# Linear attention and two mixtures of experts in one kernel: reciprocals' copies on VectorE, short tiles behind the queries' turn, and the rounding of weights spread and moved at the end of the attention

## Chip, core and metric

The kernel runs on one core of a Trainium2 chip. Its engines are TensorE (PE, with its weight loads as PEld), VectorE (DVE), ScalarE (ACT) and GpSimd (POOL); SyncE (SP) issues transfers. Each engine works through its own instructions in order and waits by semaphores for the others. The metric is the device time of one execution in microseconds, the median of several runs; less is better.

## What is computed

Three stages follow each other: a linear attention over 4 batches, 8 heads, 576 positions and 64 dimensions; a dense layer whose hidden part is the largest of three products; and a layer of 8 experts, of which each token takes two.

```python
def phi(x):                                   # attention
    proj = np.einsum('bhsd,df->bhsf', x, w_phi)
    proj = proj - np.max(np.abs(proj), axis=-1, keepdims=True)
    return np.concatenate([np.exp(proj), np.exp(-proj)], axis=-1)
q_p, k_p = (phi(q), phi(k))
kv = np.einsum('bhsf,bhsd->bhfd', k_p, v)
num = np.einsum('bhsf,bhfd->bhsd', q_p, kv)
den = np.einsum('bhsf,bhf->bhs', q_p, np.sum(k_p, axis=2))[..., None] + 1e-06
x = num / den
...
h = np.maximum(np.maximum(x @ w1, x @ w2), x @ w3)
x = h @ w_out                                 # first layer, 512 -> 768 -> 512
...
out[mask] += top2_w[mask, k, None] * (np.maximum(x[mask] @ w1[e], 0.0) @ w2[e])
```

## The kernel before

The attention runs in 16 steps, one for two heads of one batch. A step `a` takes its keys and queries through these stations: `turn` transposes them on TensorE (L373), `raw_in` copies the result (ScalarE), `proj` multiplies by `w_phi` (L394), `peak` and `center` find and subtract the largest absolute value (VectorE, L404 and L419), `exp_k` makes the exponentials of the keys (ScalarE), `turn_q` transposes the queries' once more (L437) and `exp_q` makes theirs (L446). Then `kv_sum` (L465) adds up keys by values into one PSUM bank, `kv_out` copies it to SBUF (ScalarE, L470), `denom` (L498) and `numer` (L481) multiply it by the queries' exponentials, and `den_in`, `den_turn`, `den_inv`, `den_copy`, `den_back` and `divide` make and apply the reciprocals. The denominators come in 32 partitions for each half of the positions, and `den_copy` copies each group of reciprocals to the neighbouring group, which needs them too: four small instructions a step on ScalarE (L526).

Of each head's 576 positions 512 lie in main tiles. The other 64 of two batches share a short tile, marked "r", which is worked on in the even steps; its exponentials (L427) are used in the even step and the next.

Beside this, the weights of the first layer are rounded in 24 pieces of 128 x 512 that come from DRAM as 64-bit numbers. A piece `n` is loaded by `narrow_load` (L170, into one of two buffers that it shares with all later weights, `raw`), `narrow_mid` does two VectorE instructions (L179, L181) and one on ScalarE (`nr`, L184), `narrow_end` four on GpSimd (L192 to L195), and `narrow_out` writes it to DRAM again (L205) or, for the first block, splits it in place. `nm` has three buffers and `nr` two. `step_halves(a)` says which pieces a step takes: one each from step 1, two in steps 4, 6, ..., 14, and the rest behind the last step.

What stands where is given by hand: `at(t, f, ...)` records a call at a planned time (a step is 12.5 long), the calls are sorted by this number and made in that order, and on TensorE, VectorE, ScalarE and SP the instructions keep the order of the calls. The numbers are an order, not a wait. `period(base, a, b)` does this for the second half of step `b` and the first of `a`; the seam to the first layer is written out behind it, with `pe(duration, f, ...)` moving a clock along TensorE's work. At the seam the order is: the last two sums, `numer`, the block `first(0, 0, 0)` (12 matmuls), `denom`, `numer`, the next block, and so on; `larger` and `hidden` empty its PSUM banks (three). The weights of the next blocks are loaded by `w1_load` (L216) and split by `w1_split` into `wh` (ScalarE) and `wl` (VectorE, both in a helper, L121 and L122).

Of the kernel before, what the change touches and what calls it, by code (L numbers as in the profile page):

```python
# [12 lines left out]
I32 = mybir.dt.int32  # L13
U32 = mybir.dt.uint32
AF = mybir.ActivationFunctionType
ALU = mybir.AluOpType
# [3 lines left out]
P = 128  # L20
# [3 lines left out]
class Plan:  # L24
# [5 lines left out]
    def at(self, t, f, *x):  # L30
        self.ops.append((t, len(self.ops), f, x))
# [7 lines left out]
def tile_linear_attention__then__moe__then__noisy_top2_moe(  # L39
# [20 lines left out]
    nc = tc.nc  # L60
# [9 lines left out]
    JT = S // P  # L70
# [20 lines left out]
    at = plan.at  # L91
    st, pools = {}, {}
# [16 lines left out]
    def bank_k():  # L109
        return ps.tile([P, 512], F32, name="k", bufs=1)  # L110
# [60 lines left out]
        st["bits", n] = bits  # L171

    def narrow_mid(n):
        if ("bits", n) not in st:
            return
        bits = st["bits", n]
        low, high = bits[:, :, 0], bits[:, :, 1]
        m_ = pools["attn"].tile([P, 512], I32, name="nm", bufs=3)
        nc.vector.tensor_scalar(m_, high, 0x07ffffff, 3, op0=ALU.bitwise_and,  # L179
                                op1=ALU.logical_shift_left)  # L180
        nc.vector.scalar_tensor_tensor(m_, high, -0x40000000, m_, op0=ALU.bitwise_and,  # L181
                                       op1=ALU.bitwise_or)
        r_ = pools["attn"].tile([P, 512], I32, name="nr", bufs=2)
        nc.scalar.activation(r_, low.bitcast(U32), AF.Copy, scale=float(2.0 ** -29))  # L184
        st["nm", n] = r_, m_
# [170 lines left out]
    def heads(s):  # L356
        u, i = divmod(s, 2)
        bb, hp = divmod(u, HP)
        return u, i, bb, hp
# [93 lines left out]

    def kv_sum(s, h, part=None):
        u, i, bb, hp = heads(s)
        if h == 0 and part != 1:
            st["pkv"] = bank_k().rearrange("p (a f) -> p a f", a=4)

        order = [(sg, j) for sg in range(2) for j in range(JT)] + [(0, JT), (1, JT)]
        for sg, j in (order if part is None else order[JT:] if part else order[:JT]):  # L460
            if j < JT:
                kp, vv = kps[s][:, j % 2, 2 * h + j // 2, sg, :], tiles[s][2][:, j, h:h + 2, :]
            else:
                kp, vv = kps[u, "r"][:, h, sg, :], vls[i][:, hp, h:h + 2, :]
            nc.tensor.matmul(st["pkv"][:, 2 * h + sg, :], kp, vv.rearrange("p a d -> p (a d)"),  # L465
                             start=(j == 0 and sg == 0), stop=(j == JT and sg == 1))
# [21 lines left out]
    def quarter(h, n):  # L488
        g = 2 * h + n
        return slice(g * QD, (g + 1) * QD)  # L490
# [31 lines left out]
    def den_copy(s, n):  # L522

        rc = st["rc", s]
        for h in range(2):
            nc.scalar.activation(rc[quarter(h, 1 - n), n, :], rc[quarter(h, n), n, :], AF.Copy)  # L526

    def den_back(s, n):
        rb = ap.tile([P, NB, 32], F32, name="rb", bufs=2)
# [9 lines left out]
    NS = B * HP  # L539
    STEP = 12.5  # L540
# [35 lines left out]
    def step_halves(a):  # L576

        def count(a):
            return min(a, 1) + (a % 2 == 0 if a > 2 else 0)

        n = sum(count(i) for i in range(a))
        return range(n, n + count(a) if a < NS else len(halves))

    def period(base, a, b):

        def at(t, f, *x):
            plan.at(base + t, f, *x)

        if 0 < a < NS:
            at(0.0, fill, a)  # L590
            if a == 3:
                at(0.0, routing_loads)
            if a == 2:
                at(2.0, routing_consts)
            if a + 1 < NS:
                at(0.0, load_main, a + 1)
                at(0.0, load_vals, a + 1)
        if a < NS and a % 2 == 0:
            at(0.0, prepare, a)
        if 1 < a < NS:  # L600
            if a + 1 == 2 * HP:
                at(0.0, load_rest, 1)
            at(0.0, turn, a, "k")
            at(0.5, raw_in, a, "k")
            at(2.7, turn, a, "q")
            at(3.2, raw_in, a, "q")
            at(3.15, proj, a, "k")
            at(4.0, peak, a, "k", 0)
            at(4.7, center, a, "k", 0)
            at(5.4, peak, a, "k", 1)  # L610
            at(6.1, center, a, "k", 1)
            for g in range(2):
                for sg in range(2):
                    at(5.3 + 1.5 * g + 0.6 * sg, exp_k, a, "k", g, sg)
            at(7.25, proj, a, "q")
        if 0 < a < NS:
            at(8.1, peak, a, "q", 0)
            at(8.8, center, a, "q", 0)
            at(9.5, peak, a, "q", 1)
            at(10.2, center, a, "q", 1)  # L620
            at(9.95, turn_q, a, "q", 0)
            at(10.5, exp_q, a, "q", 0)
            at(11.05, turn_q, a, "q", 1)
            at(11.5, exp_q, a, "q", 1)
            if a % 2 == 0:
                at(2.8, turn, a, "r")
                at(3.4, raw_in, a, "r")
                at(11.4, proj, a, "r")
                for g in range(2):
                    at(11.5 + 0.01 * g, peak, a, "r", g)  # L630
                    at(11.52 + 0.01 * g, center, a, "r", g)
                at(STEP + 3.0, turn_q, a, "r", 0)
                at(STEP + 3.1, exp_q, a, "r", 0)
                at(12.39, exp_k, a, "r", 0, 0)
                at(12.39, exp_k, a, "r", 0, 1)
        if a < NS:
            for n in step_halves(a):
                at(1.8 if a > 1 else 11.0, narrow_mid, n)
                at(2.8 if a > 1 else 11.5, narrow_end, n)
                at(STEP + (1.6 if a > 1 else 9.0), narrow_out, n)  # L640
            for n in step_halves(a + 1):
                at(8.0, narrow_load, n)
            if a:
                at(10.5, kv_sum, a, 0, 0)
        if 0 < b:
            at(4.05, numer, b - 1, 1)
            at(6.9, divide, b - 1, 1)
            at(0.45, kv_sum, b, 0, 1)
            at(5.0, kv_sum, b, 1)
            if b + 1 == 2 * HP:  # L650
                at(7.3, load_rest_v, 1)
            at(7.3, kv_out, b)
        if 0 <= b:
            at(8.15, denom, b)
            at(9.1, numer, b, 0)
            at(9.15, den_in, b)
            at(10.9, den_turn, b)
            at(11.0, den_inv, b)
            for n in range(2):
                at(11.2 + 0.1 * n, den_copy, b, n)  # L660
                at(11.8 + 0.5 * n, den_back, b, n)
            at(11.9, divide, b, 0)

# [46 lines left out]
    for s in range(NS):  # L710
        period(s * STEP, s, s - 1)
    T = NS * STEP
# [470 lines left out]
    def pe(dur, f, *x):  # L1183
        at(clock[0], f, *x)
        clock[0] += dur

    def after(d, f, *x):
        at(clock[0] + d, f, *x)
# [8 lines left out]
    B0 = (NS - 1) * STEP  # L1197
    at(B0 + 10.6, open_m1)
    S_ = NS - 1
    pe(1.3, kv_sum, S_, 0, 1)  # L1200
    pe(0.96, numer, S_ - 1, 1)
    at(T + 0.3, split_x, 0, 0)
    after(0.5, divide, S_ - 1, 1)
# [8 lines left out]
    for n in range(2):  # L1212
        after(1.2 + 0.1 * n, den_copy, S_, n)
        after(1.8 + 0.5 * n, den_back, S_, n)
# [2 lines left out]
    first_pe(0, 0, 1)  # L1217
    pe(0.96, numer, S_, 1, bank_p)
    after(0.6, divide, S_, 1)
    for n in step_halves(NS):  # L1220
        at(T + 3.5, narrow_mid, n)
        at(T + 4.5, narrow_end, n)
        at(T + 11.0, narrow_out, n)
    END = clock[0] + 1.9
    at(END, open_rest)
    at(END + 1.6, routing_split)
    for i in range(2 * 4):
        g, j = 1 + i // 4, i % 4
# [230 lines left out]
```

## Time and profile before

| | |
|---|---|
| median of 3 runs | 1028.51 us (1027.62 to 1028.98) |
| the profiled execution, whole | 1027.36 us |
| its span, first to last instruction | 1025.8 us |
| TensorE busy | 999.5 us, 97% of the span |
| VectorE, ScalarE, GpSimd busy | 483.1, 380.8, 336.4 us |
| mean granted TensorE clock | 0.992 of full speed |

Times in the profile run from the first instruction. The attention's steps fill the time to about 217 us, one step takes 13 to 14 us. Busy time of matmuls includes the end of their pipeline, so neighbours overlap. A row of the timeline has the start, the busy time, the engine, the line, what is written and read, how many instructions of the kind follow each other, and in brackets the idle time before it with whom it waited for. A row of a stretch has its bounds and length, then busy us and number of instructions of PE, PEld, DVE, ACT and POOL, the granted clock, the share of the DMA engines and GB/s.

### The profile page before, as it was taken

How to read it: one execution, taken by the hardware profiler on the slowest of the kernel's cores; microseconds unless marked ns; L12 is line 12 of the kernel's file. 1: busy time of each engine (PE TensorE's matmuls, PEld its weight loads, DVE VectorE, ACT ScalarE, POOL GpSimd, SP SyncE). 2: the span in 40 equal slices, each digit the busy share in tenths (PEclk: the TensorE clock that was granted, in tenths of full speed). 3: DMA queues.
4: the chain of work that ended last, by engine and by line, in shares of the span. 5: the costliest groups of instructions: out<-in, count | busy, mean ns of one | idle time of the engine just before them, and what ended most of it. 6: DMA issues, size and time to landing. Idle time of an engine off the chain costs nothing. (4 is left out here: it accounts for less than half of the span.)

```text
span 1025.8 us, 16323 instructions
## 1 busy us (share of the span) xinstructions
PE 999.5 (97%) x6429; PEld 874.1 (85%) x6429; DVE 483.1 (47%) x962; ACT 380.8 (37%) x733; POOL 336.4 (33%) x385
## 2 busy tenths in 40 slices
PE   9999999969999999999999999999999999999995
PEld 7777777749999999999998789898898979898883
DVE  5777777755342423334255536444454434444220
ACT  6677666643231313122234424333231413233110
POOL 2677655551002020202032646142332415151301
PEclk9999999989999999999999999999999999999998
DMA  7546765425000000000225347354253535352200
GB/s 196 145 132 167 217 185 170 124 73 154 21 32 1 31 1 32 1 31 1 73 68 182 79 141 253 130 155 145 92 165 98 165 117 185 113 175 80 75 19 31
DMA packets 78592, 109.25 MB, mean 106 GB/s; under 512 B 33422, under 2 KB 47886, under 8 KB 78514
## 3 DMA queue, kind: packets, MB, share of 16 engines
q1 hardware_dynamic: 67586, 78.57, 25.7%
q0 software_dynamic: 10928, 29.62, 8.7%
q8 instruction: 51, 0.84, 0.4%
q14 instruction: 27, 0.22, 0.1%
HBM read 84.77 MB, written 23.98 MB: 106 GB/s over the span
## 5 line engine op out<-in xcount | busy, mean ns | idle before, releaser
L993 PE MATMUL s<-gx,wh 128*128 128x304 f32 (+1 forms) x960 | 209.2, 309 | 0.1
L993 PEld LDWEIGHTS s<-gx,wh 128*128 128x128 f32 x960 | 159.0, 188 | 3.7 <-DVE gx L122 0.6
L993 PE MATMUL s<-gx,wl 128*128 128x304 f32 (+1 forms) x480 | 148.2, 309 | 0.0
L745 PE MATMUL s<-xh,wh 128*128 128x384 f32 x432 | 147.5, 341 | 0.0
L745 PE MATMUL s<-xh,wl 128*128 128x384 f32 x432 | 145.4, 337 | 0.0
L745 PE MATMUL s<-xl,wh 128*128 128x384 f32 x432 | 145.2, 336 | 0.0
L1081 POOL DMA_INDIRECT out_dram<-o,emeta x40 | 43.2, 1079 | 245.4 <-DVE o L1079 235.2
L922 POOL DMA_INDIRECT meta<-mt,si x36 | 35.4, 984 | 258.9 <-DVE a L755 247.8
L755 DVE TENSOR_TENSOR a<-s,a 128x384 f32<-128x384 f32 x72 | 40.1, 557 | 151.6 <-PE s L745 145.1
L1003 ACT ACTIVATE hh<-s 128x304 fp32r<-128x304 f32 (+1 forms) x120 | 52.3, 435 | 155.5 <-PE s L993 139.8
L1004 DVE SCALAR_TENSOR_TENSOR hl<-s,hh 128x304 fp32r<-128x304 f32 (+1 forms) x120 | 58.3, 488 | 100.4 <-ACT hh L1003 83.6
L122 DVE TENSOR_TENSOR wl<-raw,wh 128x1024 fp32r<-128x1024 f32 x72 | 88.1, 1224 | 36.3 <-ACT wh L121 35.6
L121 ACT ACTIVATE wh<-raw 128x1024 fp32r<-128x1024 f32 x72 | 76.0, 1056 | 55.5 <-DMA raw<-in_moe_w_dram 20.4
L993 PEld LDWEIGHTS s<-gx,wl 128*128 128x128 f32 x480 | 90.6, 189 | 1.4
L1071 PE MATMUL p<-wh,hh 128*128 128x512 f32 (+1 forms) x216 | 87.0, 403 | 0.0
L1071 PE MATMUL p<-wl,hh 128*128 128x512 f32 (+1 forms) x216 | 85.0, 394 | 0.0
L1071 PE MATMUL p<-wh,hl 128*128 128x512 f32 (+1 forms) x216 | 84.9, 393 | 0.0
L745 PEld LDWEIGHTS s<-xh,wh 128*128 128x128 f32 x432 | 81.1, 188 | 2.9 <-issue 0.5
L745 PEld LDWEIGHTS s<-xl,wh 128*128 128x128 f32 x432 | 81.2, 188 | 1.5
L745 PEld LDWEIGHTS s<-xh,wl 128*128 128x128 f32 x432 | 81.1, 188 | 0.0
L465 PEld LDWEIGHTS k<-vt,kp 128*128 128x128 f32 x512 | 60.8, 192 | 6.9 <-issue 6.5
L465 PE MATMUL k<-vt,kp 128*128 128x128 f32 x512 | 66.4, 278 | 0.1
(221 smaller groups left out, 1740.9 us busy)
## 6 DMA issues: line engine op xcount, KB each, us to landing
raw<-in_moe_w_dram SPq DMA_DIRECT2D x64, 512.0 KB, 3.5
bits<-in_moe_w_dram SPq DMA_DIRECT2D x18, 512.0 KB, 4.2
out_dram<-zrow SPq DMA_DIRECT2D x9, 512.0 KB, 5.2
x2d<-x SPq DMA_DIRECT2D x18, 256.0 KB, 2.1
km<-in_k_dram SPq DMA_DIRECT2D x16, 256.0 KB, 5.1
qm<-in_q_dram SPq DMA_DIRECT2D x16, 256.0 KB, 5.1
vt<-in_v_dram SPq DMA_DIRECT2D x32, 128.0 KB, 4.8
narrow<-nm SPq DMA_DIRECT2D x16, 256.0 KB, 3.4
```

What stands on the lines that cost most here:

```text
L121: nc.scalar.activation(hi, src, AF.Copy)
L122: nc.vector.tensor_tensor(lo, src, hi.bitcast(F32), op=ALU.subtract)
L465: nc.tensor.matmul(st["pkv"][:, 2 * h + sg, :], kp, vv.rearrange("p a d -> p (a d)"), start=(j == 0 and sg == 0), stop=(j == JT and sg == 1))
L745: nc.tensor.matmul(p_, a[:, d, fs], b_, start=(n == 0), stop=(n == 3 * KD - 1))
L755: nc.vector.tensor_tensor(a, p_, st.pop("a"), op=ALU.max)
L922: ins = nc.gpsimd.indirect_dma_start(out=meta, out_offset=bass.IndirectOffsetOnAxis(ap=si[:, t, kk:kk + 1], axis=0), in_=mt[:, t, kk, :], ...
L993: nc.tensor.matmul(p_, a[:, fs], b_[:, d, cs], start=(d == 0 and i == 0), stop=(d == KD - 1 and i == 2))
L1003: nc.scalar.activation(hh[:, cs], p_, AF.Relu)
L1004: nc.vector.scalar_tensor_tensor(hl[:, cs], p_, 0.0, hh[:, cs].bitcast(F32), op0=ALU.max, op1=ALU.subtract)
L1071: nc.tensor.matmul(p_, a[:, cs], b_[:, fw], start=(f == 0 and r == 0), stop=(f == F2 - 1 and r == 2))
L1081: alone(e, nc.gpsimd.indirect_dma_start(out=out, out_offset=bass.IndirectOffsetOnAxis(ap=mt[:m, i, 1:2], axis=0), in_=o[:m], in_offset=Non ...
```

## The change

Four edits. `den_copy` runs on VectorE, all four copies directly behind the reciprocal. `kv_sum` of the first head is cut in three, and the part over the short tiles moves behind the turn of the queries. Where a step takes two pieces, the second's `narrow_mid` is cut in two: one VectorE instruction at 7.6, the other and ScalarE's at 11.15, GpSimd's part behind it, the write-out at 4.0 of the next step. Step 15 takes two pieces as well, so that two are left for the seam, and these stand at 5.5 and 6.5 behind the last step's end, behind the last sums and their copy, where three stood at 3.5.

```diff
--- before.py
+++ after.py
@@ -171,13 +171,22 @@
         st["bits", n] = bits
 
     def narrow_mid(n):
+        narrow_high(n)
+        narrow_low(n)
+
+    def narrow_high(n):
         if ("bits", n) not in st:
             return
-        bits = st["bits", n]
+        m_ = pools["attn"].tile([P, 512], I32, name="nm", bufs=3)
+        nc.vector.tensor_scalar(m_, st["bits", n][:, :, 1], 0x07ffffff, 3, op0=ALU.bitwise_and,
+                                op1=ALU.logical_shift_left)
+        st["nh", n] = m_
+
+    def narrow_low(n):
+        if ("nh", n) not in st:
+            return
+        bits, m_ = st["bits", n], st.pop(("nh", n))
         low, high = bits[:, :, 0], bits[:, :, 1]
-        m_ = pools["attn"].tile([P, 512], I32, name="nm", bufs=3)
-        nc.vector.tensor_scalar(m_, high, 0x07ffffff, 3, op0=ALU.bitwise_and,
-                                op1=ALU.logical_shift_left)
         nc.vector.scalar_tensor_tensor(m_, high, -0x40000000, m_, op0=ALU.bitwise_and,
                                        op1=ALU.bitwise_or)
         r_ = pools["attn"].tile([P, 512], I32, name="nr", bufs=2)
@@ -453,11 +462,12 @@
 
     def kv_sum(s, h, part=None):
         u, i, bb, hp = heads(s)
-        if h == 0 and part != 1:
+        if h == 0 and not part:
             st["pkv"] = bank_k().rearrange("p (a f) -> p a f", a=4)
 
         order = [(sg, j) for sg in range(2) for j in range(JT)] + [(0, JT), (1, JT)]
-        for sg, j in (order if part is None else order[JT:] if part else order[:JT]):
+        cuts = (0, JT, 2 * JT, len(order))
+        for sg, j in order if part is None else order[cuts[part]:cuts[part + 1]]:
             if j < JT:
                 kp, vv = kps[s][:, j % 2, 2 * h + j // 2, sg, :], tiles[s][2][:, j, h:h + 2, :]
             else:
@@ -523,7 +533,7 @@
 
         rc = st["rc", s]
         for h in range(2):
-            nc.scalar.activation(rc[quarter(h, 1 - n), n, :], rc[quarter(h, n), n, :], AF.Copy)
+            nc.vector.tensor_copy(rc[quarter(h, 1 - n), n, :], rc[quarter(h, n), n, :])
 
     def den_back(s, n):
         rb = ap.tile([P, NB, 32], F32, name="rb", bufs=2)
@@ -576,7 +586,7 @@
     def step_halves(a):
 
         def count(a):
-            return min(a, 1) + (a % 2 == 0 if a > 2 else 0)
+            return min(a, 1) + (a % 2 == 0 or a == NS - 1 if a > 2 else 0)
 
         n = sum(count(i) for i in range(a))
         return range(n, n + count(a) if a < NS else len(halves))
@@ -634,7 +644,13 @@
                 at(12.39, exp_k, a, "r", 0, 0)
                 at(12.39, exp_k, a, "r", 0, 1)
         if a < NS:
-            for n in step_halves(a):
+            for i, n in enumerate(step_halves(a)):
+                if i:
+                    at(7.6, narrow_high, n)
+                    at(11.15, narrow_low, n)
+                    at(11.3, narrow_end, n)
+                    at(STEP + 4.0, narrow_out, n)
+                    continue
                 at(1.8 if a > 1 else 11.0, narrow_mid, n)
                 at(2.8 if a > 1 else 11.5, narrow_end, n)
                 at(STEP + (1.6 if a > 1 else 9.0), narrow_out, n)
@@ -646,6 +662,7 @@
             at(4.05, numer, b - 1, 1)
             at(6.9, divide, b - 1, 1)
             at(0.45, kv_sum, b, 0, 1)
+            at(2.75, kv_sum, b, 0, 2)
             at(5.0, kv_sum, b, 1)
             if b + 1 == 2 * HP:
                 at(7.3, load_rest_v, 1)
@@ -657,7 +674,7 @@
             at(10.9, den_turn, b)
             at(11.0, den_inv, b)
             for n in range(2):
-                at(11.2 + 0.1 * n, den_copy, b, n)
+                at(11.05, den_copy, b, n)
                 at(11.8 + 0.5 * n, den_back, b, n)
             at(11.9, divide, b, 0)
 
@@ -1197,7 +1214,8 @@
     B0 = (NS - 1) * STEP
     at(B0 + 10.6, open_m1)
     S_ = NS - 1
-    pe(1.3, kv_sum, S_, 0, 1)
+    for part in (1, 2):
+        pe(0.65, kv_sum, S_, 0, part)
     pe(0.96, numer, S_ - 1, 1)
     at(T + 0.3, split_x, 0, 0)
     after(0.5, divide, S_ - 1, 1)
@@ -1217,10 +1235,10 @@
     first_pe(0, 0, 1)
     pe(0.96, numer, S_, 1, bank_p)
     after(0.6, divide, S_, 1)
-    for n in step_halves(NS):
-        at(T + 3.5, narrow_mid, n)
-        at(T + 4.5, narrow_end, n)
-        at(T + 11.0, narrow_out, n)
+    for i, n in enumerate(step_halves(NS)):
+        at(T + 5.5 + i, narrow_mid, n)
+        at(T + 6.5 + i, narrow_end, n)
+        at(T + 11.0 + i, narrow_out, n)
     END = clock[0] + 1.9
     at(END, open_rest)
     at(END + 1.6, routing_split)
```

What this does to the order of the instructions shows at three places (line numbers of the changed kernel are 9 to 17 higher, and it has the names of before).

TensorE from the end of step 4 into step 5: the short tile's projection, the turn of the keys, the sums, the turn of the queries, and `turn_q` of the short tile. Before:

```order
L394 MATMUL p<-wphi,th 128x128 x4
L373 MATMUL t<-ident,km 128x128 x4
L465 MATMUL k<-vt_109,kp_872 128x128 x4
L465 MATMUL k<-vl_111,kp_965 128x128 x2
L373 MATMUL t<-ident,qm 128x128 x4
L437 MATMUL t<-ident,d 128x128 x2
L394 MATMUL p<-wphi,th 128x128 x8
```

After:

```order
L403 MATMUL p<-wphi,th 128x128 x4
L382 MATMUL t<-ident,km 128x128 x4
L475 MATMUL k<-vt_109,kp_863 128x128 x4
L382 MATMUL t<-ident,qm 128x128 x4
L475 MATMUL k<-vl_111,kp_965 128x128 x2
L446 MATMUL t<-ident,d 128x128 x2
L403 MATMUL p<-wphi,th 128x128 x8
```

The two sums over the short tiles (`vl`) stand behind the turn of the queries (`qm`); nothing else moves on TensorE.

ScalarE at the seam: `qp` is `exp_q` of step 15, `xh` the split of the first layer's input, `nr` the pieces, `kv` the copy of the last sums, `a` the emptying of the first block, `dn` the denominators. Before:

```order
L446 ACTIVATE qp_2485<-t 128x2x256 x2
L526 ACTIVATE rc<-rc 32x9 x4
L446 ACTIVATE qp_2485<-t 128x2x256 x2
L121 ACTIVATE xh<-xT 128x768 x2
L184 ACTIVATE nr<-bits 128x512 x3
L470 ACTIVATE kv<-k 128x512
L753 ACTIVATE a_2892<-s 128x384
L506 ACTIVATE dn<-t 128x288
```

After:

```order
L455 ACTIVATE qp_2485<-t 128x2x256 x2
L193 ACTIVATE nr<-bits 128x512
L455 ACTIVATE qp_2485<-t 128x2x256 x2
L121 ACTIVATE xh<-xT 128x768 x2
L480 ACTIVATE kv<-k 128x512
L193 ACTIVATE nr<-bits 128x512
L770 ACTIVATE a_2880<-s 128x384
L193 ACTIVATE nr<-bits 128x512
L516 ACTIVATE dn<-t 128x288
```

The three `nr` ahead of `kv` are gone: one (piece 21) stands between the two pairs of `exp_q`, two behind `kv`. The copies `rc` are gone.

VectorE in the second half of a step with two pieces and a short tile (step 8): `xT` is `divide`, then `peak` and `center` of the queries, the transpose and reciprocal of the denominators, and `peak` and `center` of the short tile (128x2). Before:

```order
L536 TENSOR_TENSOR xT<-s,rb 128x288
L404 TENSOR_REDUCE m<-p 128x4
L419 TENSOR_TENSOR d<-p,m 128x512
L404 TENSOR_REDUCE m<-p 128x4
L419 TENSOR_TENSOR d<-p,m 128x512
L513 STREAM_TRANSPOSE dt<-dn 128x288
L519 RECIPROCAL rc<-dt 128x18
L404 TENSOR_REDUCE m<-p 128x2 x2
L419 TENSOR_TENSOR d<-p,m 128x2x128 x2
L530 STREAM_TRANSPOSE rb<-rc 128x288
```

After:

```order
L546 TENSOR_TENSOR xT<-s,rb 128x288
L181 TENSOR_SCALAR nm<-bits 128x512
L413 TENSOR_REDUCE m<-p 128x4
L428 TENSOR_TENSOR d<-p,m 128x512
L413 TENSOR_REDUCE m<-p 128x4
L428 TENSOR_TENSOR d<-p,m 128x512
L523 STREAM_TRANSPOSE dt<-dn 128x288
L529 RECIPROCAL rc<-dt 128x18
L536 COPY rc<-rc 32x9 x4
L190 SCALAR_TENSOR_TENSOR nm<-bits,nm 128x512
L413 TENSOR_REDUCE m<-p 128x2 x2
```

The second piece's first instruction stands behind `divide`, its second behind the four copies and ahead of the short tile's `peak`.

On SP the loads of pieces 22 and 23 stand together ahead of the write-outs of pieces 20 and 21, these ahead of the first `w1_load`, and those of 22 and 23 behind the second. On GpSimd the four instructions of a piece follow each other; before, those of two pieces were interleaved.

## Rows read from the trace of the kernel before

**Rows 1.** Busy time by stretch; columns explained above:
```profile
220.00:232.50 12.50, 4.78 (x30) 2.35 (x31) 3.48 (x7) 3.17 (x9) 12.00 (x10) 0.73 0.36 106
...
245.00:300.00 55.00, 55.00 (x303) 51.62 (x302) 22.64 (x39) 19.15 (x30) 0.00 (x0) 1.00 0.17 55
```
**Rows 2.** Waits of TensorE: for whom, us in all, times, longest:
```profile
PE t L498 <- ACT kv L470: 8.2, 1, 8.2
...
PE k L465 <- ACT kp L427: 3.3, 7, 0.5
...
PE t L373 <- ACT qp L446: 0.6, 1, 0.6
```
**Rows 3.** Waits of TensorE's weight loads, same columns:
```profile
PEld t L373 <- ACT qp L446: 2.0, 7, 0.8
```
**Rows 4.** TensorE in time order, 208 to 232: start, busy us, [idle before]:
```profile
208.27 1.18 PE L498 MATMUL s<-qp,kv 128*32 128x288 f32 x16
...
210.50 0.66 PE L437 MATMUL t<-ident,d 128*128 128x128 f32 x4
...
217.13 0.42 PE L745 MATMUL s<-xh,wh 128*128 128x384 f32 x1
...
219.16 0.34 PE L745 MATMUL s<-xh,wl 128*128 128x384 f32 x1
...
227.72 2.15 PE L498 MATMUL t<-qp,kv 128*32 128x288 f32 x16 [8.23 <-ACT kv L470]
...
231.51 0.45 PE L745 MATMUL s<-xh,wh 128*128 128x384 f32 x1
```
**Rows 5.** ScalarE in order of time, 226 to 228:
```profile
226.53 0.67 ACT L184 ACTIVATE nr<-bits 128x512 int32<-128x512 uint32 x1 [9.49 <-POOL nm L195]
227.10 0.57 ACT L470 ACTIVATE kv<-k 128x512 f32<-128x512 f32 x1
```
**Rows 6.** SP's queue in order of time, 205 to 222:
```profile
205.51 16.22 SPq L170 DMA_DIRECT2D bits<-in_moe_w_out_dram  x2
```
**Rows 7.** TensorE in order of time, steps 10 and 11:
```profile
139.15 1.47 PE L394 MATMUL p<-wphi,th 64*128 64x128 f32 x16
...
147.35 0.80 PE L465 MATMUL k<-vl,kp 128*128 128x128 f32 x4 [0.47 <-ACT kp L427]
147.99 0.60 PE L373 MATMUL t<-ident,qm 128*128 128x128 f32 x4
148.42 0.38 PE L437 MATMUL t<-ident,d 128*128 128x128 f32 x2
...
153.37 1.16 PE L394 MATMUL p<-wphi,th 64*128 64x128 f32 x16
```
**Rows 8.** ScalarE in order of time, end of step 10:
```profile
144.57 0.88 ACT L526 ACTIVATE rc<-rc 32x9 f32<-32x9 f32 x4
...
146.88 0.72 ACT L427 ACTIVATE kp<-d 128x256 f32<-128x256 f32 x2 [0.32 <-DVE d L419]
```
**Rows 9.** VectorE in order of time, step 10:
```profile
133.84 0.69 DVE L181 SCALAR_TENSOR_TENSOR nm<-bits,nm 128x512 int32<-128x512 int32 x1
...
134.90 1.79 DVE L181 SCALAR_TENSOR_TENSOR nm<-bits,nm 128x512 int32<-128x512 int32 x1
...
143.69 0.27 DVE L519 RECIPROCAL rc<-dt 128x18 f32<-128x18 f32 x1
...
145.43 0.76 DVE L404 TENSOR_REDUCE m<-p 128x2 f32<-128x256 f32 x2 [1.47 <-PE p L394]
```
**Rows 10.** GpSimd in order of time, step 10:
```profile
134.87 1.27 POOL L192 TENSOR_TENSOR nm<-nm,nr 128x512 int32<-128x512 int32 x1 [7.15 <-ACT nr L184]
```
**Rows 11.** VectorE in order of time, in the routing:
```profile
354.57 0.31 DVE L873 MAX8 mx<-nl 128x8 f32<-128x8 f32 x3
```
**Rows 12.** VectorE in order of time, behind the seam:
```profile
245.65 1.23 DVE L122 TENSOR_TENSOR wl<-raw,wh 128x1024 fp32r<-128x1024 f32 x1 [0.39 <-ACT wh L121]
```
**Rows 13.** TensorE in order of time, behind the seam:
```profile
249.68 0.34 PE L745 MATMUL s<-xh,wh 128*128 128x384 f32 x1
```

## Prediction

> **What bounds the kernel now.** I read the stretches first. From 245 to 300 us TensorE is busy for 55.00 of 55.00 us at granted clock 1.00; from 220 to 232.5 us it is busy for 4.78 of 12.50 at 0.73 [rows 1]. So TensorE sets the time, and what a change can give is TensorE's idle time. The waits come next, since they say who ends it: one of 8.2 us, where the denominators' matmuls (L498) wait for the `kv` copy on ScalarE (L470), then seven of 0.5 (3.3 in all), where the sums over the short tiles (L465) wait for exponentials (L427), and one of 0.6 at a transpose of queries (L373) [rows 2]. The weight loads show seven waits at the same transposes, 2.0 us in all and 0.8 at most [rows 3]. Then I read each place in order of time.
>
> *The seam behind the last step.* TensorE runs `first(0, 0, 0)` from 217.13, starts its last matmul at 219.16, and starts the denominators only at 227.72 [rows 4]. ScalarE shows why: behind two `nr` (L184) it stands for 9.49 us until GpSimd's L195 frees a buffer for the third, and the `kv` copy is queued behind that, at 227.10 [rows 5]. The third piece's load is late, too: two loads of pieces stand in SP's row from 205.51 for 16.22 us, since the second needs the buffer that GpSimd has yet to read [rows 6].
>
> *The steps.* In step 11 the short tiles' matmuls wait 0.47 us at 147.35, behind exponentials that start at 146.88 and take 0.72; the transposes of queries follow only at 147.99 [rows 7, 8]. The exponentials wait for VectorE, which reads the projection at 145.43, as soon as TensorE has it [rows 9]. The queries' projection takes 1.47 us in step 10 (139.15) and 1.16 in step 11 (153.37) [rows 7]: step 10 rounds two pieces at its start, and VectorE's second L181 takes 1.79 us where the first took 0.69 [rows 9], so the PSUM banks come free late.
>
> **The change part by part.**
>
> *Last pieces behind the last sums.* Two pieces are left instead of three, and both of their ScalarE steps stand behind the `kv` copy. That copy takes 0.57 us [rows 5] and can start when the sums end, at about 217.2, while TensorE has a block of 2.4 us to run (217.13 to 219.16 + 0.34) [rows 4]. So the denominators find `kv` ready, and the wait of 8.2 goes. Denominators and first numerators take 2.23 us in a normal step (208.27 to 210.50) and took 3.79 here (227.72 to 231.51) [rows 4]: the granted clock had fallen in the gap. With no gap I take the normal step's time, 1.56 less. Together **9.8 us**.
>
> What is late next? Piece 23 loads once GpSimd has read piece 21, which by the plan's times comes 4.85 us earlier than now (11.15 of step 15 instead of 3.5 behind its end). ScalarE's and VectorE's queues then hold piece 23 in front of the denominators' copy, the copies of reciprocals and `larger`. TensorE needs none of these before it has run two more blocks and both numerators, some 8 us on (2.23 + 2 × 2.4 + half of 2.23), so I cost them at nothing; with that cover gone it is the second rival.
>
> *Short tiles behind the queries' turn.* The exponentials end where they did (their chain, from TensorE's projection through VectorE, is not touched), so the short tiles start at 147.35 as now; but the transposes, 0.43 us (147.99 to 148.42) [rows 7], run before that, in the wait. Seven odd steps × 0.43 = **3.0 us**. The bound above: the wait of 0.47 and the slow pace behind it (0.80 against 0.60 for four such matmuls) less 0.43 is 0.24 a step, 1.7 us more, if the exponentials came earlier as well.
>
> *Second piece in two parts.* In steps 4 to 14 the second piece's two VectorE instructions leave the start of the step. The first goes where VectorE waits for TensorE anyway. Without the second L181 (1.79) VectorE reaches the keys' projections earlier, and the queries' projection should take 1.16 instead of 1.47: 0.3 × 6 = **1.8 us**.
>
> The second L181 moves to the end of the step, between the reciprocals and the read of the short tiles' projection, together with the four copies. There VectorE is idle for 1.47 us, 143.96 to 145.43 [rows 9]. No row shows these copies on VectorE. From below, three MAX8 of 8 columns take 0.31 [rows 11], so four copies 0.4; from above, the reciprocal of the same tile takes 0.27 [rows 9], so 1.07. I take 0.7: the copies have 9 columns, nearer to the MAX8, but ScalarE's four took 0.88 [rows 8]. With 0.69 for L181 that is 1.39 of 1.47, and it fits. At the upper end it is 0.29 too long, × 6 steps = 1.7 us lost. An L181 of 1.79 would be worse by 1.1 in each, but that one began 0.03 us behind a GpSimd instruction of 1.27 (134.87) [rows 9, 10]; four such instructions for the first piece are over by about 140, so I leave that out of the steps.
>
> [...]
>
> *Copies off ScalarE.* 0.88 us [rows 8] leave ScalarE in front of the second `exp_q`, whose end frees the bank for the transposes of queries. TensorE comes to these earlier by four short matmuls, about as long as the four transposes (0.43). So the waits of [rows 3] go: six of 0.2 in even steps, of which I count 0.13 each, since a late weight load is partly hidden by the matmul before (bounds 0 and 0.2), **0.8 us**; in step 2, 0.6 + 0.43 - 0.88 = 0.15 is left of 0.6, which gives **0.45**.
>
> *A loss.* Piece 21's GpSimd work now runs beside VectorE's `split_x`, whose result TensorE reads from 217.13. The row of 1.79 prices such a meeting at 1.1 us for one instruction, 1.3 if a whole GpSimd instruction (1.27) has to pass; below it is nothing, as the split's second half is read half a block (1.2 us) later. I take **0.3**.
>
> [...]
>
> *Sum.* 9.8 + 3.0 + 1.8 + 0.8 + 0.45 - 0.3 = 15.5 us. The profiled execution took 1027.36 (span 1025.8 and 1.56 around it): 1011.8. The median of the runs is 1.15 above it, so I predict **1013.0**.
>
> **The rivals.**
>
> 1. *VectorE late at the end of the even steps.* Copies and L181 take over 1.47 us, the exponentials slip, and the wait at the short tiles grows by as much. For it: 95% of the room is used. Against: L181's price is known, only the copies are open. At their upper bound 1.7 us are lost; with GpSimd in the way in two or three steps as well, 3.5: 1014.7 to 1016.5. Chance 0.13.
>
> 2. *The seam gives part back later.* The second block of first-layer weights is loaded through the buffers that the pieces leave. Now `wl` of its third matrix runs from 245.65 for 1.23 and TensorE reads it from 249.68: 2.8 us in hand [rows 12, 13]. TensorE comes 9.8 us earlier against the pieces. The `wl` step's place in VectorE's queue is behind `larger`, which TensorE paces, and the loads behind piece 21 start about 4.85 us sooner. If only the 4.85 came, TensorE would wait 9.8 - 4.85 - 2.8 = 2.2 us; if nothing, 7.0: 1015 to 1020. Chance 0.10.
>
> 3. *The 8.2 us move to another place,* so that the change doesn't do what it says: ScalarE stands at piece 21's step inside step 15, in front of the second `exp_q`, because the piece's load or buffer is late. Half of the 9.8 or all of it would be lost: 1018 to 1023. Against: its two `nr` buffers are freed by pieces 19 and 20, rounded a step earlier or at the step's start. Chance 0.04.
>
> 4. *Slower.* SP's queue now has the write-outs of pieces 20 and 21 in front of the first load of the second block, and those of 22 and 23 in front of the third; each waits for a GpSimd chain of four instructions, 5 us by [rows 10]. It decides where the third `wl` ends 8.5 us later than it would if it only moved with the steps (15.5 less the 7.0 of rival 2). I see it sooner instead. 1028.5 to 1033. Chance 0.02.
>
> **How the numbers follow.** 0.71 for the forecast, whose own range is 1010.8 (exponentials earlier, no loss at the split) to 1014.7. The runs before differ by 1.4 us, so about 0.2% (2 us) can be told from no change. The range takes in rival 1 and the cheap half of rival 2: 1010 to 1017. Faster by over 0.2%: 0.96; within: 0.02; slower: 0.02.
>
> **What would show it.** In the changed profile: no wait of L498 for `kv`, and full granted clock from 217 to 245; the short tiles' matmuls still waiting, now behind the transposes, by under 0.3 us, seven times; all queries' projections at 1.16; no wait of transposes for `qp` from step 4 on; copies of 0.1 to 0.27 each on VectorE, and the read of the short tiles' projection still led by a wait for TensorE. The prediction is wrong if TensorE waits for `wl` behind the seam, if it waits for `xl` before `first(0, 0, 0)`, or if VectorE has no idle time before that read.

## The result and the profile after

The changed kernel takes **1013.24 us** (median of 4 runs, 1013.14 to 1014.97) where the kernel before takes 1028.45 on the same chip: ratio 0.9857, 95% interval 0.984 to 0.9874. The profiled execution took 1013.31 us (span 1011.8), 14.05 less than the one of before. The mean granted clock is 0.996.

The waits of TensorE, same columns as [rows 2]:

```profile
PE k L584 <- DVE warm L560: 1.3, 1, 1.3
PE t L382 <- DMA ql<-in_q_dram: 0.8, 1, 0.8
PE p L403 <- ACT th L392: 0.6, 1, 0.6
PE s L762 <- DVE a L772: 0.3, 1, 0.3
PE k L475 <- ACT kp L436: 0.2, 1, 0.2
```

The 8.2 us for `kv` are gone, and of the 3.3 for the short tiles' exponentials 0.2 are left as idle time of the matmuls. Their weight loads still wait seven times, 2.3 us in all, so this wait is shorter and not gone. The first three lines belong to the opening, which no edit touches. New is a wait for VectorE at L762, behind the seam.

The seam on TensorE, in order of time as [rows 4], and two stretches as in [rows 1]:

```profile
211.92 0.61 PE L475 MATMUL k<-vl,kp 128*128 128x128 f32 x4
212.29 0.42 PE L762 MATMUL s<-xh,wh 128*128 128x384 f32 x1
...
214.32 0.34 PE L762 MATMUL s<-xh,wl 128*128 128x384 f32 x1
214.58 1.18 PE L508 MATMUL t<-qp,kv 128*32 128x288 f32 x16
215.69 1.19 PE L491 MATMUL t<-qp,kv 128*64 128x288 f32 x8
216.81 0.44 PE L762 MATMUL s<-xh,wh 128*128 128x384 f32 x1
```
```profile
217.00:245.00 28.00, 27.71 (x153) 25.72 (x153) 20.18 (x31) 10.39 (x15) 10.33 (x11) 1.00 0.53 155
...
245.00:300.00 55.00, 55.00 (x306) 51.56 (x305) 21.17 (x62) 15.65 (x27) 6.36 (x6) 1.00 0.06 23
```

The denominators follow the first block at once. From the block's first matmul to the next block's it is 4.52 us (212.29 to 216.81), before 14.38 (217.13 to 231.51 in [rows 4]): **9.86 us gained**, at a granted clock of 1.00 (from 212.29 to 216.81, and in both stretches).

The steps on TensorE, VectorE and ScalarE, steps 10 and 11, to be held against [rows 7 to 9]:

```profile
136.31 1.16 PE L403 MATMUL p<-wphi,th 64*128 64x128 f32 x16
...
141.55 0.71 PE L403 MATMUL p<-wphi,th 64*128 64x128 f32 x8
142.19 0.66 PE L382 MATMUL t<-ident,km 128*128 128x128 f32 x4
...
143.58 0.60 PE L382 MATMUL t<-ident,qm 128*128 128x128 f32 x4
144.27 0.80 PE L475 MATMUL k<-vl,kp 128*128 128x128 f32 x4
145.06 0.44 PE L446 MATMUL t<-ident,d 128*128 128x128 f32 x2
```
```profile
141.03 0.70 DVE L536 COPY rc<-rc 32x9 f32<-32x9 f32 x4
141.75 0.69 DVE L190 SCALAR_TENSOR_TENSOR nm<-bits,nm 128x512 int32<-128x512 int32 x1
142.35 0.75 DVE L413 TENSOR_REDUCE m<-p 128x2 f32<-128x256 f32 x2
...
216.57 1.29 DVE L181 TENSOR_SCALAR nm<-bits 128x512 int32<-128x512 int32 x1 [2.60 <-POOL nm L201]
217.90 0.98 DVE L190 SCALAR_TENSOR_TENSOR nm<-bits,nm 128x512 int32<-128x512 int32 x1
...
219.60 3.37 DVE L536 COPY rc<-rc 32x9 f32<-32x9 f32 x4
...
225.15 0.54 DVE L772 TENSOR_TENSOR a<-s,a 128x384 f32<-128x384 f32 x1
```
```profile
143.80 0.72 ACT L436 ACTIVATE kp<-d 128x256 f32<-128x256 f32 x2 [0.86 <-DVE d L428]
144.43 0.58 ACT L392 ACTIVATE th<-t 128x512 f32<-128x512 f32 x1
```

Two stretches, the four copies in step 10 and at the seam, columns as in [rows 1] (the fifth pair is GpSimd's):

```profile
141.03:142.44 1.41, 1.41 (x16) 1.12 (x15) 1.35 (x6) 1.41 (x4) 0.00 (x0) 1.00 1.15 288
219.60:222.97 3.37, 3.37 (x22) 2.91 (x19) 3.31 (x4) 1.06 (x1) 3.26 (x3) 1.00 0.38 134
```

Three things are to be seen. The queries' projection takes 1.16 in an even step too (in step 6 alone it takes 1.35). The four copies take 0.70, as the prediction took them, and VectorE comes to the short tile's projection (142.35) without any idle time: the room is used up to the end. And at the seam the same four copies take 3.37 us; GpSimd is at work there from 215.18 to 225.9, while it rests during the copies of step 10. VectorE is late with `larger` (225.15), and TensorE waits for a bank. TensorE's lead over the kernel before falls there from 14.70 us (216.81 against 231.51) to 14.16 behind 225.2: **0.54 us given back**, 0.3 of it idle and the rest a slower start (the first matmul behind the wait takes 0.45, those behind it 0.34).

### The profile page after: what moved, and what is told of

It reads as the page before. It is cut to its first block, busy times and chain, and to the rows that moved or that the text cites. A ratio compares the mean times of both kernels' runs of the same rounds, so it can differ in the third digit from the quotient of the medians.

```text
span 1011.8 us, 16317 instructions
## 1 busy us (share of the span) xinstructions
PE 995.8 (98%) x6429; PEld 871.8 (86%) x6429; DVE 495.5 (49%) x1026; ACT 365.7 (36%) x669; POOL 337.7 (33%) x385
## 5 line engine op out<-in xcount | busy, mean ns | idle before, releaser
L1010 PE MATMUL s<-gx,wh 128*128 128x304 f32 (+1 forms) x960 | 209.2, 309 | 0.1
L1010 PEld LDWEIGHTS s<-gx,wh 128*128 128x128 f32 x960 | 158.9, 188 | 3.7 <-DVE gx L122 0.6
L1010 PE MATMUL s<-gx,wl 128*128 128x304 f32 (+1 forms) x480 | 148.2, 309 | 0.0
L762 PE MATMUL s<-xh,wh 128*128 128x384 f32 x432 | 147.6, 342 | 0.3 <-DVE a L772 0.3
L762 PE MATMUL s<-xh,wl 128*128 128x384 f32 x432 | 145.4, 337 | 0.0
L762 PE MATMUL s<-xl,wh 128*128 128x384 f32 x432 | 145.2, 336 | 0.0
L1010 PEld LDWEIGHTS s<-gx,wl 128*128 128x128 f32 x480 | 90.6, 189 | 1.4
L762 PEld LDWEIGHTS s<-xh,wh 128*128 128x128 f32 x432 | 81.1, 188 | 3.5 <-issue 0.9
L762 PEld LDWEIGHTS s<-xl,wh 128*128 128x128 f32 x432 | 81.2, 188 | 1.5
L762 PEld LDWEIGHTS s<-xh,wl 128*128 128x128 f32 x432 | 81.1, 188 | 0.0
```

The costliest lines, as they stand in the source:

```text
L762: nc.tensor.matmul(p_, a[:, d, fs], b_, start=(n == 0), stop=(n == 3 * KD - 1))
L1010: nc.tensor.matmul(p_, a[:, fs], b_[:, d, cs], start=(d == 0 and i == 0), stop=(d == KD - 1 and i == 2))
```

## The experiments

Each was timed beside the kernel before, whose medians were 1027.8 to 1028.1 us there. In the result it took 1028.45, so a difference to the changed kernel is uncertain by about half a microsecond. Since the parts lie in repeated steps, I also give the length of an even and an odd step, from one turn of keys (L373, then L382) to the next, steps 10 and 11 of each trace. A trace is of one execution; those of runs 2 and 7 took 2.4 us more than their medians, with waits in the expert layer (L1010), far behind these steps. The diffs are shown in part.

| kernel | median, us | turns of keys at | even step | odd step |
|---|---|---|---|---|
| before | 1028.45 | 131.64, 145.33, 158.53 | 13.69 | 13.20 |
| changed | 1013.24 | 129.09, 142.19, 155.22 | 13.10 | 13.03 |
| 1 last pieces early | 1022.10 | 128.96, 142.06, 155.09 | 13.10 | 13.03 |
| 2 copies on ScalarE | 1018.67 | 132.33, 146.12, 159.36 | 13.79 | 13.24 |
| 3 short sums ahead | 1014.57 | 129.65, 142.76, 156.00 | 13.11 | 13.24 |
| 4 second piece whole | 1020.99 | 134.51, 148.01, 161.58 | 13.50 | 13.57 |
| 5 before + copies on VectorE | 1032.56 | 135.28, 148.78, 162.57 | 13.50 | 13.79 |
| 9 second piece: VectorE early | 1018.01 | 132.51, 146.01, 159.11 | 13.50 | 13.10 |
| 10 = 2 and 4 together | 1016.94 | 131.79, 145.58, 158.55 | 13.79 | 12.97 |
| 7 copy-out first | 1011.57 | 127.97, 141.08, 153.89 | 13.11 | 12.81 |
| 8 = 7 and short sums later | 1010.56 | 127.53, 140.69, 153.27 | 13.16 | 12.58 |

**The theory** was that the four edits add up, each by its term of the sum. **The rival**, from rival 1 and the 3.37 us above: the copies on VectorE are cheap only while GpSimd rests, so copies and the cut of the second piece are worth something only together.

**1. Last pieces early** (undone alone: `count` without step 15, the loop at 3.5 as before).

```diff
-        at(T + 5.5 + i, narrow_mid, n)
+        at(T + 3.5, narrow_mid, n)
```

> The changed kernel, with the last three pieces back at 3.5 behind step 15, ahead of the copy of the last sums. By the prediction's term for the seam (9.8) it takes 1013.2 + 9.8 = 1023.0 us and TensorE waits some 8 us for kv again. By the trace of the changed kernel, where the seam itself gained 9.86 and gave 0.54 back at the emptying of a bank at 225 us (the wait for larger), it takes 1013.2 + 9.3 = 1022.5. If the steps had gained more than it seems and the seam less, as rival 2 or 3 had it, it comes out under 1021.

1022.10 us, ratio 0.9944 (0.993 to 0.9957), 8.9 us over the changed kernel. ScalarE, in order of time:

```profile
220.72 0.67 ACT L193 ACTIVATE nr<-bits 128x512 int32<-128x512 uint32 x1 [9.49 <-POOL nm L204]
221.29 0.58 ACT L480 ACTIVATE kv<-k 128x512 f32<-128x512 f32 x1
```

The wait of [rows 5] is back with the same 9.49 us. The steps are as long as in the changed kernel, so the seam's gain stands by itself, at 9.86 less the 0.54 given back. Against the kernel before, timed beside each, the gains are 15.21 and 5.86, which puts the seam at 9.35.

**2. Copies on ScalarE.**

```diff
-            nc.vector.tensor_copy(rc[quarter(h, 1 - n), n, :], rc[quarter(h, n), n, :])
+            nc.scalar.activation(rc[quarter(h, 1 - n), n, :], rc[quarter(h, n), n, :], AF.Copy)
```

> The changed kernel, with the four copies of reciprocals on ScalarE again, at their old place. By the prediction's terms for them (0.8 + 0.45) it takes 1014.5 us. By the trace of the changed kernel they are worth more: in even steps TensorE came to the transposes 0.29 us sooner and not 0.13, and in odd steps the transposes of queries now stand directly behind the keys' sums, at 143.58 where the second exp_q ends at 142.94; 0.88 us of copies ahead of it would end it at 143.8. That gives 1.7 in even steps, about 0.25 x 7 in odd ones, 0.5 in step 2, less 0.5 at the seam, where the copies on VectorE take 3.37 us beside GpSimd: 1016.6. If rival 1 was at work (VectorE late by the copies), it is no slower than 1013.2.

1018.67 us, ratio 0.9909 (0.9894 to 0.9924): 5.4 over the changed kernel, more than any reading gave. ScalarE at the end of step 10, and TensorE behind it:

```profile
145.23 0.66 ACT L193 ACTIVATE nr<-bits 128x512 int32<-128x512 uint32 x1
145.92 0.88 ACT L536 ACTIVATE rc<-rc 32x9 f32<-32x9 f32 x4
146.83 1.08 ACT L455 ACTIVATE qp<-t 128x512 f32<-128x512 f32 x2
```
```profile
147.96 0.66 PE L382 MATMUL t<-ident,qm 128*128 128x128 f32 x4 [0.29 <-ACT qp L455]
```

The copies and the second piece's `nr`, which the cut put there, stand ahead of the second `exp_q`. The transposes of queries, moved up by the edit that run 3 undoes, wait for its end: 13 times, 5.6 us in all. The price depends on the other edits.

**3. Short sums ahead.**

```diff
-            at(2.75, kv_sum, b, 0, 2)
+            at(0.46, kv_sum, b, 0, 2)
```

> The changed kernel, with the sums over the short tiles ahead of the queries' transposes again. By the prediction's term (7 x 0.43) it takes 1016.2 us. By the trace of the changed kernel an odd step gained only 0.17 us, since the exponentials come 0.06 later and the next transposes then wait for ScalarE: 7 x 0.17 = 1.2, 1014.4. If a part of the even steps' gain is also its doing (the short sums took 0.45 us there, not 0.63), it is up to 1.1 more: 1015.5.

1014.57 us, ratio 0.987 (0.9855 to 0.9885): 1.3 over. An odd step is 0.21 longer, an even one not, so the edit is worth 7 x 0.2 and not 7 x 0.43.

**4. Second piece whole** (at 1.8, in steps 4 to 14).

```diff
-                if i:
+                if i and a == NS - 1:
```

> The changed kernel, with the second piece of the even steps 4 to 14 rounded at the step's start again (step 15 left as changed). By the prediction's term (6 x 0.3) it takes 1015.0 us and the queries' projection 1.40 us again in the even steps. By the trace of the changed kernel the same 1.7 comes back, but VectorE is no longer 0.06 us late at the short tile's projection, 7 x 0.06 = 0.4: 1014.5. By rival 1 (VectorE has no room at the end of the even steps) the latter is larger and the kernel is about as fast as the changed one, 1013 to 1013.5.

1020.99 us, ratio 0.9933 (0.9919 to 0.9947): **7.7 us over**, four times the term. VectorE, GpSimd and TensorE at the end of step 10:

```profile
146.67 1.89 DVE L536 COPY rc<-rc 32x9 f32<-32x9 f32 x4
148.59 0.76 DVE L413 TENSOR_REDUCE m<-p 128x2 f32<-128x256 f32 x2
```
```profile
145.51 1.49 POOL L203 TENSOR_SCALAR nr<-nr 128x512 f32<-128x512 f32 x1
147.08 1.27 POOL L204 TENSOR_TENSOR nm<-nm,nr 128x512 f32<-128x512 f32 x1
```
```profile
150.63 0.79 PE L475 MATMUL k<-vl,kp 128*128 128x128 f32 x4 [0.64 <-ACT kp L436]
```

With both pieces started early GpSimd is still at its last two instructions of them when the copies come. They take 1.89 instead of 0.70, the exponentials slip, and the odd step is 0.54 longer.

**5. Copies alone, on the kernel before.**

```diff
-                at(11.2 + 0.1 * n, den_copy, b, n)
+                at(11.05, den_copy, b, n)
```

(with the copy on VectorE as in the change)

> The kernel before, with its copies of reciprocals on VectorE and nothing else changed. By the prediction's terms (0.8 + 0.45, the copies fitting into the 1.47 us of room) it gains 1.25: 1026.7 us against some 1028.0. By the theory that GpSimd holds up such copies (0.95 to 1.24 us for one instead of 0.16, as at 219.6 us in the changed kernel and in the run with the second piece whole, where four took 1.89), they meet the two pieces' eight GpSimd instructions, which are over only after 145 us in step 10: about 1.9 us for four in 1.47 of room, 0.45 late in six steps, 2.7 lost against 1.4 gained: 1029.3, with VectorE not waiting for TensorE ahead of the short tile's read.

1032.56 us, ratio 1.0044 (1.003 to 1.0057): this edit alone makes the kernel **slower by 4.4 us**. Its four copies at the end of step 10, on VectorE:

```profile
147.44 1.89 DVE L526 COPY rc<-rc 32x9 f32<-32x9 f32 x4
149.36 0.76 DVE L404 TENSOR_REDUCE m<-p 128x2 f32<-128x256 f32 x2
```

The direction was expected, the size was not: steps 4 and 6 are 0.9 longer as well (14.58 against 13.66 and 13.65). In them GpSimd also splits the first block's weights. In step 4 the split starts 2.35 us behind the turn of keys here, and 3.19 before, so the second piece's first instruction now meets it and takes 1.50 us instead of 0.42:

```profile
53.38 1.50 DVE L179 TENSOR_SCALAR nm<-bits 128x512 int32<-128x512 int32 x1
```

Run 9 shows the same meeting with its effect on TensorE.

**6. GpSimd's part late.** The VectorE and ScalarE instructions at 1.8 again, `narrow_end` left at 11.3.

> The changed kernel, with the second piece's two VectorE instructions and ScalarE's at the start of the even steps 4 to 14 again, but its GpSimd part left behind the copies, where the change put it. If the run with the whole second piece lost its 7.7 us because GpSimd was still at work when the copies came, the copies take 0.71 again and only the queries' projection is late (0.3 to 0.4 in six steps), less 0.06 x 6 since the second instruction no longer stands ahead of the short tile's read: 1014.5 to 1015.5. If the VectorE instructions at the step's start cost the 7.7 themselves, it takes 1020 to 1021.

1021.66 us, ratio 0.9939 (0.9925 to 0.9952). The edit missed its aim: GpSimd's instructions do not keep the order of the calls, and the trace has its two chains interleaved as in run 4, with copies of 1.88. It decides nothing, and run 9 took its place.

**9. VectorE's part early, ScalarE's late.** Since GpSimd's first instruction needs `nr`, this holds GpSimd back.

```diff
-                    at(7.6, narrow_high, n)
-                    at(11.15, narrow_low, n)
+                    at(1.8 if a < NS - 1 else 7.6, narrow_high, n)
+                    at(1.8 if a < NS - 1 else 11.15, narrow_low, n)
+                    at(11.15, narrow_scalar, n)
```

> The changed kernel, with the second piece's two VectorE instructions at the start of the even steps 4 to 14 again, but ScalarE's instruction left at 11.15, so that GpSimd cannot start the second chain before the copies are past. If the copies' meeting with GpSimd is what made the whole second piece cost 7.7 us, the four copies take 0.71 again in the even steps, the read of the short tile's projection is not late, and only the queries' projection is (0.40 us in six steps), less 6 x 0.06: 1015 us (1014.5 to 1016). If it is the second L190 at the step's start that costs the 7.7, through what it makes late, it takes 1020 to 1021 with copies of 0.71.

1018.01 us, ratio 0.9903 (0.9888 to 0.9918): between the two. The copies are quick again and the odd step is 13.10, so of the 7.7 us the held copies cost about 3.0 (1020.99 less 1018.01; `nr` and GpSimd's chain come later here too, so the copies aren't the only difference). The other 4.8 are mostly VectorE's, at the start of the even steps. In step 6, VectorE and then TensorE:

```profile
80.94 1.50 DVE L182 TENSOR_SCALAR nm<-bits 128x512 int32<-128x512 int32 x1
82.48 1.64 DVE L191 SCALAR_TENSOR_TENSOR nm<-bits,nm 128x512 int32<-128x512 int32 x1
```
```profile
86.91 1.13 PE L410 MATMUL p<-wphi,th 64*128 64x128 f32 x14 [0.86 <-DVE d L435]
```

Both instructions meet GpSimd, which in steps 4 and 6 also splits the first block's weights: the first starts inside the split (1.68 us from 80.48), the second inside the next GpSimd instruction (1.45 from 82.12). TensorE's queries' projection waits, and those two steps are 1.4 longer than in the changed kernel. The other four even ones are 0.4 longer, which I had expected of all six.

**10. Copies on ScalarE and the second piece whole** (the diffs of 2 and 4).

> The changed kernel with two edits undone together: the copies on ScalarE, and the second piece whole at the start of the even steps. Undone alone they cost 5.4 and 7.7 us. If the 7.7 are mostly copies that GpSimd holds up, they vanish with the copies on ScalarE, and only the queries' projection is left (6 x 0.31 = 1.9 over the 1018.7 of copies on ScalarE alone): 1020.5 us. If the two costs are independent, they add to 1026.3.

1016.94 us, ratio 0.9893 (0.9877 to 0.9908): 3.7 over the changed kernel, **less than either undone alone** (5.4 and 7.7). TensorE and VectorE in step 12:

```profile
160.57 0.66 PE L382 MATMUL t<-ident,qm 128*128 128x128 f32 x4 [0.47 <-ACT qp L455]
...
166.46 1.16 PE L403 MATMUL p<-wphi,th 64*128 64x128 f32 x16
```
```profile
161.82 1.80 DVE L190 SCALAR_TENSOR_TENSOR nm<-bits,nm 128x512 int32<-128x512 int32 x1
```

With the copies on ScalarE TensorE waits for the second `exp_q` in the even steps. This time covers VectorE's second piece, although its L190 is longer: it takes 1.74 to 1.82 in five of the six even steps and 0.69 in step 10, and all six are 13.79 long, with the queries' projection at 1.16. A whole second piece then costs nothing. Cutting it (run 2) only puts an `nr` ahead of `exp_q`: 0.27 in each odd step, 1.7 us. So on top of the other two edits each of the pair alone loses (copies alone 4.1, from 1016.94 to 1020.99; the cut alone 1.7), and both together gain 3.7.

**7 and 8. What was left in the odd steps.** In the changed kernel `turn_q` of the short tile (145.06) starts as ScalarE's copy of the transposed keys ends (144.43 + 0.58), and that stands behind the exponentials, though ScalarE is idle for 0.86 us ahead of them. Run 7 turns the two round; run 8 also moves the short sums behind `turn_q`.

```diff
-                at(12.39, exp_k, a, "r", 0, 0)
-                at(12.39, exp_k, a, "r", 0, 1)
+                at(STEP + 0.55, exp_k, a, "r", 0, 0)
+                at(STEP + 0.55, exp_k, a, "r", 0, 1)
-            at(2.75, kv_sum, b, 0, 2)
+            at(3.05, kv_sum, b, 0, 2)
```

> The changed kernel, with the short tile's exponentials on ScalarE behind the copy of the transposed keys instead of ahead of it, where ScalarE stands idle for 0.86 us in the odd steps. If the transposes of the short tile (turn_q) wait for that copy, as the weight loads show (seven times up to 0.2), an odd step gets 0.15 to 0.2 shorter: 7 x 0.17 = 1.2, 1012.0 us. If they wait for the exponentials' own chain, nothing changes: 1013.2.

> The run before this one (copy of the transposed keys first), and the sums over the short tiles one place further back, behind turn_q of the short tile. If what is left of the wait is the exponentials' alone (0.26 us behind the transposes of queries), turn_q's 0.37 us covers it: 7 x 0.26 = 1.8 more, 1010.2 us and no wait of these sums at all. If turn_q itself cannot start earlier than the sums (its input is ready at 143.76, TensorE there at 144.01), it stays at 1012.

Run 7: 1011.57 us, ratio 0.9838 (0.9825 to 0.9852). Run 8: **1010.56 us**, ratio 0.983 (0.9817 to 0.9844), faster than both kernels; no wait for these exponentials is left. TensorE in run 8:

```profile
142.07 0.60 PE L382 MATMUL t<-ident,qm 128*128 128x128 f32 x4
142.51 0.38 PE L446 MATMUL t<-ident,d 128*128 128x128 f32 x2
142.75 0.79 PE L475 MATMUL k<-vl,kp 128*128 128x128 f32 x4
```

Each took some 0.22 off an odd step. The even steps, where there is nothing to cover, got 0.05 longer.

**11 and 12. Further corrections.** Both put the last step's copies on ScalarE, and the short sums behind `turn_q` where `b` is odd. Run 11 also moves the second piece's L190 behind the short tile's reads.

```diff
+            if s == NS - 1:
+                nc.scalar.activation(rc[quarter(h, 1 - n), n, :], rc[quarter(h, n), n, :], AF.Copy)
-            at(2.75, kv_sum, b, 0, 2)
+            at(3.05 if b % 2 else 2.75, kv_sum, b, 0, 2)
-                    at(11.15, narrow_low, n)
-                    at(11.3, narrow_end, n)
+                    at(11.6, narrow_low, n)
+                    at(11.7, narrow_end, n)
```

> The changed kernel with what the runs so far gave: the copy of the transposed keys ahead of the short tile's exponentials on ScalarE, the short sums behind turn_q in odd steps alone, the copies of the last step on ScalarE (where GpSimd is at work), and the second piece's L190 behind the short tile's reads on VectorE. From 1010.6 us: 0.54 at the seam (no wait of L762 for the emptying by VectorE, copies 0.9 and not 3.4), 6 x 0.05 in even steps, and 6 x 0.06 for reads that are not late: 1009.4. If L190 behind the reads delays the division and through it a bank of TensorE's, it is slower than the run beside it.

> As the run before, but with L190 left ahead of the short tile's reads: 0.54 and 6 x 0.05 from 1010.6 us, 1009.8. Between this and the run before lies the 0.06 us by which VectorE reads late in the even steps: 0.4 at most.

Run 12: 1011.31 us, ratio 0.9838 (0.9825 to 0.9852). The wait of L762 is gone. But the sums of `b` run while step `b + 1` begins, so `b` odd hit the even steps, and what run 8 gains in the odd ones is missing (12.80 in step 11 of run 12). Run 8 with the last step's copies on ScalarE wasn't run. Run 11: 1023.78 us, ratio 0.9958 (0.9945 to 0.9972), 12.5 slower than run 12. ScalarE and TensorE in it:

```profile
73.06 0.63 ACT L219 ACTIVATE wh<-nm 128x512 fp32r<-128x512 f32 x1 [4.85 <-POOL nm L204]
```
```profile
75.78 2.15 PE L508 MATMUL s<-qp,kv 128*32 128x288 f32 x16 [2.89 <-ACT kv L480]
```

L190 comes late, GpSimd's chain starts late, and ScalarE stands at the split of that piece with the keys' exponentials and the `kv` copy queued behind: two steps of 17.6 us. It is the seam's stall again, in another place, for the sake of 0.06 us.

## Why the prediction was right, point by point

The median was met within 0.24 us (1013.0 against 1013.24). The sum behind it was not that good: the profiled executions differ by 14.05 us where 15.5 was forecast. The 1.15 us from profile to median, added for before, isn't there after (1013.31 against 1013.24), and this covered most of the difference. To that extent the last digits are luck. The errors of the terms, too, cancel in part: 9.86 - 0.54 + 1.2 + 3.3 + 0.52 - 0.3 makes the 14.05.

- *The seam* (9.8): 9.86. The mechanism was shown by run 1.
- *What is late next at the seam* (cost: nothing): 0.54. The prediction named the queue, piece 23 ahead of copies and `larger`, and called some 8 us of TensorE's work cover enough. It left out that the copies and L181 (1.29 for 0.39) would run beside GpSimd; runs 2 and 12, with the last copies on ScalarE, have no such wait, though L181 takes 1.24 in run 12 too. So the copies make it.
- *Short tiles behind the queries' turn* (3.0): about 1.2, the sum over the seven odd steps. This is the term that was mis-sized. The exponentials didn't end where they did: VectorE reads 0.80 after the projection's start (141.55 to 142.35), before 0.74. And behind the sums `turn_q` met a wait for ScalarE that the old order had covered (its weight loads wait seven times, 1.3 us in all); runs 7 and 8 took both out.
- *Second piece* (1.8) *and copies off ScalarE in even steps* (0.8): 3.3 together, summed over the six even steps; the queries' projection gave 0.31 of 0.59 in step 10, and the earlier turn of the queries ahead of it 0.28, where the prediction counted 0.13 for it. Right as a pair, and sized too low. As two separate terms they don't exist: runs 2, 4 and 10 show that either alone makes the kernel slower, and the prediction's sum had no place for that. Step 2 (0.45): 0.52.
- *Loss at the split* (0.3): none; TensorE doesn't wait for `xl`.
- The rest, 0.3, was lost in the opening (0.16 up to step 2) and behind the seam (0.11), and no edit explains it.
- The lower end of the forecast's own range, 1010.8, doesn't follow from the two terms that it names: 1013.0 - 1.7 - 0.3 is 1011.0.

Rival 1 was near. The prediction said that no idle time ahead of the short tile's read would prove it wrong. From step 4 on there is none, so by this sign its claim that the work fits was wrong, though it cost only 0.06 us a step. The copies at 0.70 and L190 at 0.69 filled the room to the end, and they weren't longer because GpSimd is quiet at that moment (0.00 us busy from 141.03 to 142.44). Run 4 shows the copies with GpSimd in the way, which rival 1 priced at up to 3.5 us: about 3.0, with L190 elsewhere. Of the other signs, one more failed in one place: the projection of step 6 took 1.35, behind an L181 of 1.39 that met GpSimd's split. Rivals 2 to 4 did not come: TensorE nowhere waits for `wl` behind the seam.

## What to carry to other kernels

Where one engine's instructions take longer while another works, as these copies do (0.16 us or up to 1.24), test edits in pairs: of two edits here each lost alone and both together gained 3.7 us. Before a small instruction moves to another engine, look at what the neighbour engines do at that moment, not only at whether the new engine is idle. And an engine that waits in its order for a slow side chain holds up all that is queued behind it (ScalarE for 9.49 us at the seam of before, for 4.85 in run 11), so work of that kind goes behind what the bounding engine needs next, with its inputs long ready.

## What the runs showed of the hardware

In the changed kernel a copy of 32 x 9 takes 0.16 to 0.17 us on VectorE, and 0.45 to 1.24 (six of seven over 0.9) when it starts during a GpSimd instruction of 1.0 to 1.3. It ends as that instruction ends: the longest, from 220.60, at 221.84, GpSimd's at 221.81. All 64 copies of the changed kernel, shortest, median and longest in ns:

```profile
L536 DVE COPY rc<-rc x64: 159/166/1237, 24.5 to 222.0; 32x9 f32<-32x9 f32 x64
```

L181, one input and 0.39 us, takes 1.39 in step 6 of the changed kernel, from 79.22, inside a GpSimd instruction of 1.27 from 79.05, and 1.50 in run 9, from 80.94, inside the one of 1.68 from 80.48; each ends 0.28 behind GpSimd's. But of the 17 L181 that start inside a GpSimd instruction in the changed kernel only two take over 1 us (1.29 and 1.39), the others 0.38 to 0.59. The reductions of 128 x 512 from PSUM (L413) stay at 0.68 to 0.69 there, also the 44 of 64 that start inside a GpSimd instruction. The reciprocals (0.26 to 0.27) and VectorE's transposes (L523 and L540, 0.46 to 0.48), which read SBUF, were not held either, also where they lay inside a GpSimd instruction (4 of 16 and 19 of 48 start in one). What decides which of VectorE's instructions are held, no trace shows.

In a step in which GpSimd rests the four copies follow each other by 0.17 to 0.20 us at 0.16 to 0.17 each, so they don't overlap; in step 10 the four take 0.70.
